# A fused attention and mixing kernel on one core: first loads in two-token runs by halves of the heads, gates eight deep in batch 1, and a new order of instructions

## The chip, the cores and the metric

The kernel runs on one core of one Trainium2 chip. The metric is the device time of one execution in microseconds, with the median of several runs. The profile shows a span that is 1.7 to 1.8 us shorter than this time. All profiles used below are of runs with a granted TensorE clock of 0.995 to 1.0 of full speed.

## The reference, cut to what matters

```python
scores = q @ k.T / sqrt(64) - slope[h] * dist        # 4 batches, 8 heads, 768 tokens, 64 wide
keep = is_global | is_local                          # 8 global tokens, 96 local ones
x = softmax(where(keep, scores, -1e9)) @ v           # heads side by side: (4, 768, 512)
theta = x @ w_theta
u = x + w_tok_r @ (x * cos(theta)) + w_tok_i @ (x * sin(theta))
out = u + relu(u @ w_ch)
```

The kernel works in tiles of 128 tokens. Two tiles make a third of a batch, so there are twelve thirds. Two heads make a pair, and a third has four pairs.

## The kernel before

The program is a table of named operations and a string `ORDER` that lists them in the order in which they are issued; each engine executes its own in that order. The names are short: `t0010` is the transpose of q or k (batch 0, third 0, k = 1, first half), `q000` and `k000` are its evictions from PSUM, `kg` and `kp` write a second copy of k, `sid` is a diagonal, `dtab` a part of the distance table, `etab` a bias table made from it, `bi` the bias matmul of one head, `s` is a pair's scores, `x` the exponential of one head, `v` the product with v, `th` theta, `mx` the token mixing, `ch` the channel mixing. A suffix such as `/ACT` names the engine; `+27` asks for 27 filler matmuls ahead of the operation.

```python
def fill(p_, acc=False):                       # fillers: multiply zeros while TensorE would wait
    for _ in range(plan.pad):
        ...
def load(fn, us, ndesc, spot, depth=0, ...):   # loads with a cast are issued by GpSimd
    ...
    if depth:                                  # the gate: read one element of the load depth back
        add(f"gate{n}", {"POOL": 0.35},
            lambda: nc.gpsimd.tensor_copy(out=scrap, in_=landed[n - depth]()), ...)
    add(f"load{n}", ...)
def first(i, t):                               # q and k of the first third: f32, from SP and ACT
    a = new(st, "e", [T, H, D], FP)
    (nc.sync, nc.scalar)[i].dma_start(out=a,
        in_=(q, k)[i][0, :, t * T:(t + 1) * T, :].rearrange("h p d -> p h d"))
    ...                                        # then a cast to bf16, transposes, evictions
```

Four such first loads bring q and k of 256 tokens: one for each of q, k and tile, all eight heads. A load of one tile has 128 x 8 runs of 64 f32, which is 256 B each.

The softmax here doesn't subtract the row's maximum and nothing guards it: scores larger than these inputs give would overflow.

Of the kernel before, what the change touches and what calls it, by code (L numbers as in the profile page):

```python
# [37 lines left out]
ones6 hw00 hw10 zero rel ones3 tiny hw01 halfpi hw11 warm0 ones5 ones1 ones4 ones2 load1 ones0 ident sid0 far0  # L38
sid2 far1 load2 dtab0 dtab1 dtab2 load3 dtab3 sid4 sid5 etab7 sid1 sid6 sid7 load4 sid3 etab6 bi0000
cast00/DVE bi0001 bi0010 etab3 load5 t0000 cast10/DVE bi0011 q000/DVE etab1 t0010+5 load6 k000/DVE etab2 kg000  # L40
kp000/DVE load7 etab0 cast01/DVE etab5 t0001+27 load8 cast11/DVE etab4 q001/DVE t0011+12 load9 k001/DVE kg001
s000+3 kp001/DVE load10 s001 x0000 x0001 load11 bi0020+3 t0100 x0010 x0011 bi0021 bi0030 load12 q010/DVE t0110
bi0031 s003 k010/DVE load13 s002 x0030 kg010 kp010/DVE x0031 load14 vpa00/DVE x0020 vpb00/DVE x0021 bi0100+6
load15 v003 v000 v001 load16 bi0101 n000 s010 vpa01/DVE load17 bi0110 x0100 bi0111 vpb01/DVE s011 load18 x0101
n003 bi0120 v002 x0110 load19 n001 bi0121 s012 x0111 n002 bi0130 x0120 v010 bi0131 n010 s013 x0121 v011 x0130
v012 n011 t0200 x0131 n012 t0210 q020/ACT bi0200 k020/DVE xt00 bi0201 xc00/ACT bi0210 kp020/DVE bi0211 kg020
v013 vpa02/DVE s020 n013 s021 x0200 vpb02/DVE xt01+6 x0201 bi0220 gate20 x0210 xc01/DVE bi0221+1 load20 v020
x0211 s022 n020 tw00 gate21 x0220 v021 load21 twc00/DVE bi0230 x0221 bi0231 n021 s023 gate22 th000 x0230
load22 x0231 v022 tw10 ts0 gate23 n022 tw11 load23 v023 twc10/DVE th001 n023 gate24 twc11/ACT load24 tw01 xt02
cos000 twc01/DVE gate25 th011 sin000 load25 xc02/DVE cos001 z000 gate26 th010 load26 sin001 th020 z001 cos010  # L50
gate27 load27 sin010 th021 cos011 z010 gate28 t1000 sin011 load28 tw21 cos020 q100/DVE mx000 gate29 sin020
twc21/DVE load29 t1010 cos021 z011 gate30 mx010 sin021 k100/DVE load30 tx1 vpa10/DVE mx001 gate31 kg100 load31
vpb10/DVE z020 mx011 gate32 kp100/DVE load32 z021 tw20 s100 twc20/DVE s101 gate33 mx002 x1000 load33 x1001
x1010 mx012 u00 x1011 gate34 load34 s102 m101 s103 tw30 u01 x1020 gate35 mx020 x1021 m100 load35 x1030 m102
x1031 mx022 gate36 twc30/DVE load36 m103 mx021 gate37 load37 ut00 u02 ut01 uc00/ACT v102 gate38 t1110 uc01/DVE
load38 tw31 k110/DVE ch01 twc31/ACT gate39 kp110/DVE load39 t1100 kg110 o01 v101 v103 q110/DVE gate40 v100
st01 tw41 load40 ch00 n100 twc41/ACT n101 gate41 ut02 load41 tw40 vpa11/DVE uc02/ACT mx030 o00 twc40/ACT
gate42 vpb11/DVE load42 st00 mx032 n102 n103 mx031 gate43 load43 s110 gate44 u03 s111 load44 x1100 t1200 ch02
x1110 gate45 q120/DVE load45 x1101 ut03 x1111 t1210 m110 gate46 uc03/ACT s112 load46 m111 s113 k120/ACT mx040
o02 gate47 x1120 load47 mx041 kp120/DVE st02 x1121 kg120 gate48 x1130 tw51 m112 load48 v110 twc51/ACT tw50  # L60
n110 v111 mx042 gate49 x1131 n111 load49 twc50/ACT vpa12/DVE s120 u04 s121 gate50 x1200 mx050 load50 m113
x1210 vpb12/DVE ut04 x1201 gate51 ch03 uc04/DVE load51 x1211 m120 s122 o03 gate52 s123 x1220 mx051 load52 m121
x1230 st03 v113 x1221 gate53 xt10 n113 load53 x1231 mx052 m122 ts1 gate54 v120 load54 u05 v112 v121 v122 n112
xc10/ACT ut05 gate55 ch04 n120 load55 uc05/DVE th100 vpa20/DVE gate56 m123 load56 ch05 cos100 vpb20/DVE n121
gate57 sin100 v123 load57 xt11 n122 th101 n123 xc11/ACT gate58 load58 o04 xt12 cos101 o05 th110 st04 gate59
sin101 xc12/DVE load59 st05 th111 cos110 z100 gate60 sin110 th121 z101 load60 cos111 z110 th120 sin111 gate61
vpa21/DVE load61 z111 t2100 cos120 t2010 gate62 vpb21/DVE sin120 load62 t2000 q210/DVE cos121 mx110 z120
gate63 sin121 q200/DVE load63 mx111 k200/ACT z121 gate64 t2110 tx2 load64 kg200 mx112 kp200/DVE k210/DVE
gate65 s200 u11 load65 s201 mx100 x2000 kp210/DVE x2001 ut11 kg210 gate66 x2010 mx101 m200 load66 x2011 s202
m201 gate67 s203 t2200 vpa22/DVE load67 x2020 x2021 t2210 vpb22/DVE x2030 q220/DVE v200 gate68 mx102 x2031  # L70
load68 n200 k220/ACT s210 m203 gate69 s211 m202 load69 x2100 mx120 kp220/DVE x2101 u10 gate70 mx122 x2110
load70 m210 x2111 ut10 s212 kg220 gate71 v202 m211 v201 x2120 load71 ch11 n202 x2121 n201 gate72 v203 s213
load72 n203 mx140 x2130 m212 xt20 gate73 x2131 v210 load73 vpa30/DVE s220 n210 v211 x2200 mx121 gate74 n211
x2201 load74 vpb30/DVE s221 m220 s222 gate75 x2210 ch10 load75 u12 x2211 m213 v220 x2220 ut12 mx130 gate76
x2221 m221 load76 s223 n220 v221 gate77 x2230 m222 mx141 load77 x2231 n221 v222 ts2 gate78 v212 m223 mx131
load78 n212 v223 gate79 n222 v213 load79 mx132 n223 n213 gate80 th200 xt22 load80 o11 mx142 vpa31/DVE cos200
gate81 xt21 u13 load81 sin200 ch12 vpb31/DVE u14 gate82 th201 ut13 load82 o12 mx150 o10 cos201 ut14 z200
sin201 mx151 z201 st12 mx152 st11 th221 st10 u15 t3110 ut15 t3010 k310/DVE t3000 k300/DVE t3100 kp310/ACT
th211 q300/DVE q310/ACT kp300/DVE th210 kg300 kg310 vpa32/DVE th220 cos210 vpb32/DVE sin210 t3210 cos211 t3200
z210 ch13 k320/ACT q320/DVE mx200 sin211 kp320/DVE cos220 o13 ch14 sin220 z211 st13 cos221 mx210 z220 sin221  # L80
o14 mx201 tx3 z221 st14 s300 kg320 s301 mx202 x3000 x3010 mx212 x3001 u20 x3011 m300 s302 ut20 s303 m301 ch15
x3020 x3021 x3030 mx211 o15 x3031 s310 m303 st15 s311 u21 x3100 mx220 x3101 m302 ut21 v300 x3110 mx222 m310
x3111 n300 mx221 m311 v301 u22 v303 v302 v310 n302 ch20 ut22 n301 mx230 o20 n303 ch21 st20 n310 xt30 s312 o21
s313 x3120 mx232 x3121 st21 v311 x3130 mx231 n311 x3131 m312 s320 s321 u23 x3200 mx240 x3201 m313 ut23 v312
x3210 ch22 n312 x3211 m320 s322 s323 o22 x3220 mx241 x3230 m321 st22 v313 x3221 mx250 n313 x3231 m322 ts3 v321
xt31 v320 m323 mx252 n320 v322 v323 n321 ch23 n323 th300 n322 o23 xt32 mx242 cos300 sin300 th301 u24 st23 z300
th310 ut24 cos301 sin301 mx251 cos310 z301 th311 sin310 u25 mx300 z310 cos311 ut25 sin311 th320 z311 th321
cos320 sin320 mx301 cos321 z320 ch24 sin321 z321 mx310 o24 mx302 st24 mx312 u30 mx311 ut30 ch25 u31 mx320 ut31
o25 mx322 st25 mx321 ch30 u32 mx330 ut32 o30 mx331 st30 ch31 mx332 o31 mx340 st31 u33 mx341 ut33 mx342 ch32
u34 mx350 ut34 o32 mx352 st32 mx351 ch33 u35 ut35 o33 ch34 uc35/ACT st33 ch35 o34 ch351 o35 st34 o351 st35  # L90
# [5 lines left out]
def kernel(  # L96
# [52 lines left out]
    def act_t(n):  # L149
        return 0.06 + n * 0.00084  # L150
# [11 lines left out]
    DEPTH = 5  # L162
# [58 lines left out]
    def load(fn, us, ndesc, spot, depth=0, reads=(), writes=(), alloc=None):  # L221
        nload[0] += 1
        n = nload[0]
        landed[n] = spot
        after = [f"load{n - 1}"] if n > NFREE else ["hw00"]
        if n == NFREE + 1:
            after = [f"load{i}" for i in range(1, NFREE + 1)]
        if depth:
            add(f"gate{n}", {"POOL": 0.35},
                lambda: nc.gpsimd.tensor_copy(out=scrap, in_=landed[n - depth]()),  # L230
                reads=[("ld", n - depth)], prio=-100 + n - 0.5, after=after)
            after = [f"gate{n}"]
        add(f"load{n}", {"POOL": 0.62 + 0.00028 * ndesc}, fn, reads=reads, writes=list(writes) + [("ld", n)],
            alloc=alloc, prio=-100 + n if n > NFREE else None, lat=(1.05, us + {1: -0.12, 10: 1.1}.get(n, 0.0), 0.65), after=after)
# [39 lines left out]
    def first(i, t):  # L274
# [3 lines left out]
        def fn():  # L278
            a = new(st, "e", [T, H, D], FP)
            (nc.sync, nc.scalar)[i].dma_start(out=a, in_=(q, k)[i][0, :, t * T:(t + 1) * T, :].rearrange("h p d -> p h d"))  # L280

        add(f"hw{i}{t}", {eng: 0.5}, fn, writes=[st], alloc={st: "e"}, prio=-300 + t,
            lat=(0.9, (0.98, 0.7, 1.75, 0.88)[2 * t + i], 1.45), after=["hw00"] if i + t else [])

        def cast():
            if key not in tiles:
                new(key, "qk", [T, 2, 2, DM], BF)
            vector[o.took](out=tiles[key][:, i, t].rearrange("p (h d) -> p h d", d=D), in_=tiles[st])
# [449 lines left out]
```

## Time and profile before

| | before |
|---|---|
| median time | 174.28 us (174.23 to 174.46, 3 runs) |
| profiled span | 172.6 us |
| TensorE busy, with fillers | 162.9 us, 94% |
| VectorE, ScalarE, GpSimd busy | 133.4, 106.0, 85.0 us |
| first exponential starts | 10.39 us |
| last load issued | 100.41 us |

A timeline line has the start, the length of the group, the engine, the line of the kernel, the operation, output and inputs, the count, and in brackets how long the engine stood idle before it and what ended that.

### The profile page before, as it was taken

To read this page: it belongs to the slowest core of one execution; us is meant where nothing else is said; L and a number is where in the kernel's file an instruction comes from. 1 tells how busy PE (TensorE), PEld (TensorE's weight loads), DVE (VectorE), ACT (ScalarE), POOL (GpSimd) and SP (SyncE) were. 2 spreads that over 40 slices of the span, in tenths; PEclk is the share of its full clock that TensorE was granted. 3 is DMA by queue.
4 is the path that set the end of the run, shared out by engine and by line. 5 is a ranking of instruction groups with operands and counts; after the bars stand their busy time and mean duration, and the time that the engine had idled before them with its cause. 6 is when DMAs were issued, how large, how long until landed. Compare 5 with 4: busy or idle time off the path is not lost.

```text
span 172.6 us, 4153 instructions
## 1 busy us (share of the span) xinstructions
PE 162.9 (94%) x1598; PEld 93.2 (54%) x1623; DVE 133.4 (77%) x315; ACT 106.0 (61%) x187; POOL 85.0 (49%) x150
## 2 busy tenths in 40 slices
PE   7998999999997999999999997999999999999991
PEld 2764776555664656565555643654555644444440
DVE  7948886798897698999999994795997975634442
ACT  3954988996445888799877540799518847300010
POOL 8998249779895899898996940000000000000000
PEclk9999999999999999999999999999999999999999
DMA  5999999999999999999999999612335364134334
GB/s 121 188 154 155 188 173 123 143 165 163 157 157 178 184 119 158 113 208 129 132 131 114 165 141 177 219 65 77 105 98 139 104 95 123 48 92 133 93 91 182
DMA packets 96868, 23.73 MB, mean 138 GB/s; under 512 B 91088, under 2 KB 93904, under 8 KB 96848
## 3 DMA queue, kind: packets, MB, share of 16 engines
q0 software_dynamic: 73504, 12.33, 100.7%
q1 hardware_dynamic: 21264, 10.62, 25.1%
q10 hardware_dynamic: 2080, 0.52, 1.7%
q8 instruction: 12, 0.20, 0.5%
q14 instruction: 8, 0.07, 0.1%
HBM read 25.69 MB, written 6.29 MB: 185 GB/s over the span
## 4 chain that ended last, share of the span: by engine, by line
PE 48%; DMA 30%; POOL 6%; DVE 6%; issue 5%; ACT 2%; DVEq 0%; POOLq 0%; SPq 0%; ACTq 0%
PE pb L592 22%; DMA qk<-in_k_dram 10%; PE pb L636 9%; PE pa L549 8%; DMA w_theta_bf<-in_moe_w_theta_dram 5%; DMA qk<-in_q_dram 4%; DMA xT<-x 4%; DMA uT<-u 3%; POOL qk L243 3%; DMA w_ch_bf<-in_moe_w_ch_dram 3%; PE pa L451 3%; PE pa L504 3%; PE pb L371 2%; POOL scrap L230 1%; DVE e L482 1%
## 5 line engine op out<-in xcount | busy, mean ns | idle before, releaser
L592 PE MATMUL pb<-zri,w_tokT 128*128 128x512 bf16 x273 | 67.3, 379 | 1.1 <-issue 0.5
L474 ACT ACTIVATE e<-pa 128x512 bf16<-128x512 f32 (+1 forms) x96 | 46.5, 565 | 20.0 <-PE pa L451 19.4
L592 PEld LDWEIGHTS <-w_tokT 128*128 128x128 bf16 x288 | 26.1, 98 | 28.2
L604 DVE TENSOR_TENSOR u<-x,pb 128x512 bf16<-128x512 bf16 x24 | 16.4, 682 | 11.9 <-PE pb L592 11.7
L636 PE MATMUL pb<-w_ch_bf,uT 128*128 128x512 bf16 (+1 forms) x96 | 24.0, 370 | 0.3
L549 PE MATMUL pa<-w_theta_bf,xT 128*128 128x512 bf16 x93 | 22.5, 379 | 1.3 <-DMA xT<-x 1.1
L482 DVE TENSOR_TENSOR e<-e,etab 128x1024 bf16<-128x1024 bf16 (+1 forms) x36 | 22.4, 639 | 0.4
L257 POOL DMA_DIRECT2D vn<-in_v_dram x24 | 21.8, 910 | 1.4 <-issue 1.4
L558 ACT ACTIVATE cs<-pa,halfpi 128x512 bf16<-128x512 f32 x24 | 16.6, 693 | 9.4 <-PE pa L549 9.2
L243 POOL DMA_DIRECT2D qk<-in_q_dram x22 | 19.6, 891 | 1.9 <-issue 0.9
L570 DVE TENSOR_TENSOR zri<-x,cs 128x1024 bf16<-128x1024 bf16 x24 | 16.2, 685 | 5.0 <-ACT cs L560 4.9
L243 POOL DMA_DIRECT2D qk<-in_k_dram x22 | 19.3, 877 | 0.0
L642 DVE SCALAR_TENSOR_TENSOR o<-pb,u 128x512 f32<-128x512 f32 (+1 forms) x25 | 16.2, 663 | 3.7 <-PE pb L636 3.7
L504 PEld LDWEIGHTS <-e 128*128 128x128 bf16 x352 | 14.5, 98 | 5.2
L517 DVE TENSOR_TENSOR x<-pa,rec 128x256 bf16<-128x256 f32 x36 | 15.3, 425 | 1.2
L620 ACT COPY uT<-pb 128x512 bf16<-128x512 bf16 x4 | 2.4, 594 | 20.9 <-PE pb L616 20.9
L549 PEld LDWEIGHTS <-xT 128*128 128x128 bf16 x96 | 8.9, 98 | 11.5 <-DMA xT<-x 1.6
L371 PE MATMUL pb<-ident,qk 128*128 128x128 bf16 x192 | 14.1, 221 | 1.0 <-DMA qk<-in_k_dram 1.0
L451 PEld LDWEIGHTS <-kk 64*128 64x128 bf16 x352 | 9.9, 94 | 9.3 <-issue 8.0
L451 PE MATMUL pa<-qT,kk 64*128 64x128 bf16 x352 | 14.9, 218 | 0.0
L560 ACT ACTIVATE cs<-pa 128x512 bf16<-128x512 f32 x24 | 14.4, 602 | 0.0
L230 POOL COPY scrap<-qk 1x1 bf16<-1x1 bf16 x33 | 11.3, 343 | 5.1 <-DMA qk<-in_k_dram 2.6
(69 smaller groups left out, 207.2 us busy)
## 6 DMA issues: line engine op xcount, KB each, us to landing
out_dram<-o SPq DMA_DIRECT2D x23, 256.0 KB, 2.3
vn<-in_v_dram POOLq DMA_DIRECT2D x24, 128.0 KB, 5.4
qk<-in_q_dram POOLq DMA_DIRECT2D x22, 128.0 KB, 5.5
qk<-in_k_dram POOLq DMA_DIRECT2D x22, 128.0 KB, 5.3
w_nat<-in_moe_w_tok_r_dram POOLq DMA_DIRECT2D x6, 192.0 KB, 6.0
w_nat<-in_moe_w_tok_i_dram POOLq DMA_DIRECT2D x6, 192.0 KB, 6.5
e<-in_k_dram ACTq DMA_DIRECT2D x2, 256.0 KB, 5.8
e<-in_q_dram SPq DMA_DIRECT2D x2, 256.0 KB, 5.1
```

The lines of the kernel that those rows point to most:

```text
L243: nc.gpsimd.dma_start(out=tiles[key][:, i, t].rearrange("p (h d) -> p h d", d=D), in_=(q, k)[i][b, :, r0:r0 + T, :].rearrange("h p d -> p ...
L257: nc.gpsimd.dma_start(out=v_bufs[i][:, t, :, 0:D], in_=v[b, :, r0:r0 + T, :].rearrange("h p d -> p h d"))
L371: nc.tensor.transpose(p_[:, t - u0, p], tiles[key][:, i, t, p * T:(p + 1) * T], ident)
L451: nc.tensor.matmul(p_[hh][:, s], lhsT=tiles["kk", b, kg][R, kt, p, r, :], rhs=tiles["qT", b, g][R, qt, p, :], start=not biased, stop=not b ...
L474: nc.scalar.activation(tiles[ek][:, hh, 0:n], tiles[pb[hh]][:, 0:n], AF.Exp, scale=scale)
L482: nc.vector.tensor_mul(e_[:, :, 0:n], e_[:, :, 0:n], etab[:, 2 * p:2 * p + 2, s0:s0 + n])
L504: nc.tensor.matmul(o, lhsT=l_, rhs=r_, start=(i == 0), stop=(i == len(mms) - 1))
L549: nc.tensor.matmul(p_, lhsT=tiles["xT", b, g][:, p, t, :], rhs=w_theta_bf[:, p, :], start=(p == 0), stop=(p == NP - 1))
L558: nc.scalar.activation(tiles[ck][:, 0], tiles[ps], AF.Sin, bias=halfpi)
L592: nc.tensor.matmul(p_, lhsT=w_tokT[wi][:, 2 * g + t, tt * T:(tt + 1) * T], rhs=tiles["z", b, g][:, t, wi, :], start=(n == 1 and t == 0 and ...
L604: nc.vector.tensor_add(u.rearrange("n (p c) -> n p c", p=NP), tiles["x", b, tt // 2][:, :, tt % 2, :], tiles[ps].rearrange("n (p c) -> n p ...
L636: nc.tensor.matmul(p_, lhsT=tiles["uT", b, tt][:, p, :], rhs=w_ch_bf[:, p, i * w:(i + 1) * w], start=(p == 0), stop=(p == NP - 1))
```

## The change

Its intent is to shorten the start and to let loads run further ahead. There are four parts. First, each first load takes four heads of all 256 tokens instead of eight heads of 128, and a partition holds two neighbouring tokens, so one run is 512 B. The eviction from PSUM puts the tokens back in order. Second, gates in batch 1 look eight loads back and later gates six, where all looked five back. Third, the diagonals that add the distance bias stay on VectorE, now ahead of the distance table. Fourth, there is a new `ORDER`. Options that are off are cut.

```diff
-    DEPTH = 5
+    DEPTH = 6
+    DEPTH1 = 8
...
-            a = new(st, "e", [T, H, D], FP)
-            ...in_=(q, k)[i][0, :, t * T:(t + 1) * T, :].rearrange("h p d -> p h d"))
+            a = new(st, "e", [T, H // 2, 2 * D], FP)
+            ...in_=(q, k)[i][0, H // 2 * t:H // 2 * (t + 1), 0:2 * T, :].rearrange("h (p j) d -> p h (j d)", j=2))
...
-    batch(1, 0, 0)
-    load_w_tok(2, DEPTH)
+    batch(1, 0, 0, DEPTH1)
+    load_w_tok(2, DEPTH1)
     ... (all loads of batch 1 alike)
+            if halves:
+                vector[o.took](out=d_.rearrange("c t p (n j) -> c t p n j", j=2),
+                               in_=tiles[ps].rearrange("c p j (t n) -> c t p n j", t=2))
...
 ORDER, its start:
-sid2 far1 load2 dtab0 dtab1 dtab2 load3 dtab3 sid4 sid5 etab7 sid1 sid6 sid7 load4 sid3 etab6 bi0000
-cast00/DVE bi0001 bi0010 etab3 load5 t0000 cast10/DVE bi0011 q000/DVE etab1 t0010+5 load6 k000/DVE ...
+sid1 sid0 sid2 load2 sid5 sid6 ident far0 far1 load3 dtab0 dtab1 dtab2 load4 cast00/ACT dtab3 bi0000+1
+cast10/DVE etab5 bi0001 t0000 load5 t0010 q000/ACT bi0010 bi0011 k000/DVE load6 etab7 kg000 cast01/DVE etab4
+load7 kp000/DVE t0001+22 cast11/DVE etab1 s001 q001/DVE t0011 load8 etab0 s000 k001/DVE x0000 ...
```

## The prediction

> **What bounds the kernel now.** I read the page first: busy shares, slices, queues.
>
> ```profile
> PE 162.9 (94%) x1598; PEld 93.2 (54%) x1623; DVE 133.4 (77%) x315; ACT 106.0 (61%) x187; POOL 85.0 (49%) x150
> PE   7998999999997999999999997999999999999991
> DMA  5999999999999999999999999612335364134334
> q0 software_dynamic: 73504, 12.33, 100.7%
> ```
>
> TensorE looks full from end to end, and the DMA engines are full up to slice 25 of 40 (about 108 us) and mostly free after that. The first impression needs a correction: the order of the program holds filler matmuls (a number behind a plus sign), which multiply zeros while TensorE would wait. They count as busy. The groups by shape show them:
>
> ```profile
> L145 PE MATMUL pb<-ident,zero 128*128 128x128 bf16 x50 | 3.5, 219 | 0.0
> L147 PE MATMUL pa<-zero 128*128 128x512 bf16 x6 | 1.8, 378 | 0.5 <-ACT e L474 0.4
> L147 PE MATMUL pa<-zero 128*128 128x384 bf16 x6 | 1.3, 325 | 0.4 <-ACT e L474 0.4
> ```
>
> So I counted useful matmuls, each at the spacing that it has in back-to-back runs of the timeline: 216 ns with 512 columns (8 took 1.90 us, of which the last one's 379 ns is latency), 163 ns with 384, 108 ns with 256 (taken as half of 216), 56 ns for a 128-column transpose (27 fillers in 1.67 us), 34 ns for a score matmul (16 in 0.55 us), 30 ns with 65 columns. 492 x 216 + 8 x 163 + 8 x 108 + 340 x 56 + 352 x 34 + 352 x 30 ns = 150 us. TensorE works from 1.24 to 167.9 us, 166.7 us, so some 16 us of that are warm-up, fillers and waiting. Adding up the same products in stretches of 5 us shows where: by 30 us some 16.8 us of useful work are done, so 13 of the 16 us are lost there. After that the loss grows by about 1.5 us between 55 and 65, by 1 us between 80 and 95 and by 1 us at 105; the remainder is paid back by rounding. **The first 30 us are what can be won**, and the timelines of ScalarE and GpSimd say what limits them:
>
> ```profile
> 4.19 5.12 ACT L682 ACTIVATE etab<-dtab 128x640 bf16<-128x640 bf16 x8 [0.89 <-DVE dtab L207]
> 10.39 1.64 ACT L474 ACTIVATE e<-pa 128x384 bf16<-128x384 f32 x4 [1.07 <-PE pa L451]
> 13.43 1.64 ACT L474 ACTIVATE e<-pa 128x384 bf16<-128x384 f32 x4 [1.40 <-PE pa L451]
> 16.90 4.11 ACT L474 ACTIVATE e<-pa 128x512 bf16<-128x512 f32 x8 [1.83 <-PE pa L451]
> 20.97 1.01 ACT L380 COPY qT<-pb 128x1024 bf16<-128x1024 bf16 x1
> ...
> 18.38 0.53 POOL L269 DMA_DIRECT2D w_nat<-in_moe_w_tok_r_dram  x1 [1.83 <-DMA qk<-in_k_dram]
> 19.30 0.53 POOL L269 DMA_DIRECT2D w_nat<-in_moe_w_tok_i_dram  x1 [0.39 <-DMA qk<-in_q_dram]
> 23.48 0.18 POOL L230 COPY scrap<-w_theta_bf 1x1 bf16<-1x1 bf16 x1 [3.65 <-DMA w_theta_bf<-in_moe_w_theta_dram]
> ```
>
> ScalarE makes all eight bias tables early, then waits three times (4.3 us) for scores. The first score needs all four first loads, which here land between 4.7 and 8.05 us (the issues at line 280 took 4.0 to 6.8 us to land). GpSimd shows a limit that no gate sets: load 18 starts when load 10 has landed and load 19 when load 11 has, so eight loads are outstanding at most. Then comes the first gate, which waits 3.65 us for w_theta, because it asks for the load five before it. Last, the chain that ended last and TensorE's timeline at 55 us:
>
> ```profile
> 49.31 6.74 DMA qk<-in_k_dram
> 99.09 7.33 DMA xT<-x
> ...
> 56.10 0.40 PE L371 MATMUL pb<-ident,qk 128*128 128x128 bf16 x4 [0.97 <-DMA qk<-in_k_dram]
> ```
>
> TensorE waits 0.97 us for the last k load of batch 1, and later for a transposing DMA that shares the queue with the last loads.
>
> **What the Trainium skill says.** "DMA: Bandwidth & Descriptors", Specifications, gives 512 B as the least transfer for line rate; the old first loads move 256 B per head and token, the new ones 512 B. The trace agrees that small packets rule: 91,088 of 96,868 are below 512 B. "Perfetto Trace Analysis", Identifying the Most-Contended Engine, warns that matmul busy time is a poor measure of distance to the roofline; here 94% busy hides 16 us. "VectorE: DVE Perf Modes", Why PSUM operands drop a tier, caps a PSUM source at two elements per cycle, and What auto-detection actually checks asks for step 1 for that; the new evictions of the first third read PSUM with a step of 128 elements, so they should drop to one. In this trace 512 bf16 elements from PSUM at step 1 take 0.42 us, and 512 f32 elements from PSUM (line 642) 0.68 us.
>
> **The change part by part.**
>
> First loads. Four loads of 1,024 packets of 256 B become four of 512 packets of 512 B. In the stationary part of the stream eight loads of 1,024 packets were outstanding and each took about 8.4 us (load 10: issued 9.99, landed 18.38), so one costs the queue 1.05 us, 16.4 ns for each of 64 packets per engine. I take 0.8 us for the new form, an estimate: half the packets, each somewhat longer. Saved: 4 x 0.25 = 1.0 us; the last first load lands at 7.0 instead of 8.05, and everything behind it in the queue about 1.0 us, perhaps up to 2.0 us, sooner.
>
> Halves of the heads. Scores of head pairs 0 and 1 now need only the first q and the first k load, no longer all four. Cost: three evictions on VectorE grow from 0.42 to about 0.66 us (+0.7 us), one moves to ScalarE with one cast (+1.2 us there). The diagonals stay where they were, only earlier than the distance table, so no time comes of them.
>
> New order on ScalarE. Five tables before the first exponential, three between. Walked through with measured durations: table of distances ready on VectorE about 5.2 us, five tables 3.2 us, eviction 0.6 us: first exponential at 9.0 instead of 10.39. Its eight short exponentials (0.41 each) and three tables (0.64) fill the old waits and end near 14.3, where the exponentials of the second third start: 2.6 us before the 16.90 of now. The transposes of the last third need loads 9 to 12, which landed near 20 us and now land near 18 to 19. That caps the gain: **1.2 to 2.8 us, say 2.2, at 30 us**. The fillers say much the same: before 50 x 56 + 6 x 163 + 7 x 216 ns = 5.3 us, after 42 x 56 + 1 x 163 + 5 x 216 ns = 3.6 us, 1.7 us fewer.
>
> Gates eight deep. With eight outstanding allowed anyway, the gates of batch 1 hold nothing back: the 3.65 us behind w_theta go, and the 1.0 us behind w_ch. But the stream is limited by the queue too, so not all of it arrives: by 1.05 us per load and one load per 1.05 us, I put the last k load of batch 1 at 49 to 51 us instead of 56.05. The new order asks for it earlier: the useful work ahead of that transpose is 41.8 us before and 38.7 after. At the speed of the start it would be wanted near 50 us. So this is worth between -1.0 and +1.0 us against the start, +0.3 on average.
>
> The end of the loads (60 to 107 us). Gates of later batches are six deep instead of five, and the stream starts earlier, so the last loads should be out some 3 us sooner and the transposing DMAs near 100 us find a freer queue. Of the 1 us at 105 and the 1 us between 80 and 95 I count 0.5.
>
> Sum: 2.2 + 0.3 + 0.5 = 3.0 us, less 0.1 for small new bubbles. The measured time is 1.7 us longer than the profiled span and I leave that as it is: 174.28 - 2.9 = 171.4 us.
>
> **Rivals.** (1) The load stream binds. The start is capped by loads 9 to 12 at the 1.0 us saved and TensorE then waits at the last k load of batch 1. For it: DMA full to 108 us. Against it: only about 2 us of direct waits on loads now. It would give about 173.2. (2) VectorE binds from 60 to 105 us, where it is busy 43.3 of 45 us; moving a few copies to ScalarE and others back leaves its sum alike. An earlier start then helps only if VectorE's work of the stretch also starts earlier, which it can. Where it does not, some 1.5 us are lost again: 172.8. (3) Deeper gates lengthen each transfer: with eight outstanding a load took 8.4 us, with five 5.4. Stores and transposing DMAs between 85 and 105 us could land later with six outstanding, +0.5 to 1 us: 172.3. (4) All parts add: start 2.8, wait at 55 gone, wait at 105 gone: 169.6.
>
> **Range and chances.** Centre 171.4, with 169.6 from rival 4 and 173.2 from rival 1 as ends. Two per cent is 170.79, so 3.5 us must come; that needs the start near its upper end and one of the later waits gone, about one in three. Slower by 2% would need a new wait of 6 us beside the gain at the start: 0.03.
>
> **What would show it.** First exponential near 9.0 us and the exponentials of the second third near 14.3; waits of ScalarE for scores in the first 20 us below 1.5 us instead of 4.3; first transposes of batch 1 near 32 instead of 34.17; no wait of 3.65 us at a gate; the last k load of batch 1 landing at 49 to 51 us; evictions of the first third at about 0.66 us; the last load issued some 3 us before 100.4. The prediction is wrong if the exponentials start early but TensorE's first work of batch 1 does not, or if a wait of 2 us or more for a load stands near 50 us, or if the gain of the first 30 us is lost between 60 and 107 us.

## The result, and the profile after

The changed kernel took 171.17 us in the median (171.0 to 171.41, 4 runs), the kernel before 174.37 us (174.23 to 177.04, 4 runs) beside it. Ratios here are the mean time of one kernel's fast runs over that of the other's of the same rounds, so not quite the ratio of the medians: 0.982, interval 0.9801 to 0.9839. The run of 177.04 us counts as slow (over 1.5% above the fastest) and is left out of the ratio. The gain is clear of the noise, but by the 2% rule the verdict is "same". The output is correct and the profiled span fell from 172.6 to 169.6 us.

The same rows of the page of the changed kernel:

```profile
PE 162.1 (96%) x1581; PEld 91.9 (54%) x1608; DVE 136.0 (80%) x316; ACT 103.9 (61%) x186; POOL 80.7 (48%) x150
DMA  4999999999999999999999438303363373143334
```

TensorE is as busy as before in a shorter span. The DMA engines are full up to slice 22 (about 93 us) instead of 25. The timeline of ScalarE of the changed kernel, start and length first:

```profile
5.93 0.74 ACT L742 ACTIVATE etab<-dtab 128x640 bf16<-128x640 bf16 x1 [0.77 <-DVE dtab L211]
10.01 0.87 ACT L526 ACTIVATE e<-pa 128x384 bf16<-128x384 f32 x2 [0.36 <-PE pa L499]
14.99 1.08 ACT L526 ACTIVATE e<-pa 128x512 bf16<-128x512 f32 x2
16.34 3.25 ACT L526 ACTIVATE e<-pa 128x512 bf16<-128x512 f32 x6 [0.26 <-PE pa L499]
19.76 1.01 ACT L439 COPY qT<-pb 128x1024 bf16<-128x1024 bf16 x1 [0.17 <-PE pb L425]
```

The first bias table starts at 5.93 us, where it started at 4.19. The first exponential is only 0.38 us sooner, the second third's (14.99 for 16.90) 1.9 us sooner, and the eviction that opens the last third (19.76 for 20.97) 1.2 us sooner. GpSimd of the changed kernel, with its loads and gates:

```profile
17.94 0.53 POOL L273 DMA_DIRECT2D w_nat<-in_moe_w_tok_i_dram  x1 [1.48 <-DMA qk<-in_q_dram]
18.61 0.18 POOL L234 COPY scrap<-qk 1x1 bf16<-1x1 bf16 x1
19.04 0.90 POOL L247 DMA_DIRECT2D qk<-in_q_dram  x1 [0.26 <-issue]
42.41 0.88 POOL L247 DMA_DIRECT2D qk<-in_k_dram  x1
48.42 0.28 POOL L234 COPY scrap<-qk 1x1 bf16<-1x1 bf16 x1
86.22 0.93 POOL L261 DMA_DIRECT2D vn<-in_v_dram  x1
```

The wait of 3.65 us behind w_theta is gone: the first load of batch 1 goes out at 19.04 us, where it went at 24.11. The last k load of batch 1 goes at 42.41 instead of 49.31. The copy at 48.42 is the gate that reads this load, and it did not wait, so the load had landed by then. The last load of all is issued at 86.22 instead of 100.41 us.

Where did the 3.0 us of span come from? Three operations have the same amount of TensorE work ahead of them in both orders, so their times can be compared: the first transpose of batch 1, the last transpose of x in batch 1, and the first theta of batch 3. Their lines from the timeline, before and then after:

```profile
34.17 0.61 PE L371 MATMUL pb<-ident,qk 128*128 128x128 bf16 x8
71.77 0.61 PE L530 MATMUL pb<-ident,x 128*128 128x128 bf16 x8
138.92 1.03 PE L549 MATMUL pa<-w_theta_bf,xT 128*128 128x512 bf16 x4
```

```profile
33.09 0.61 PE L425 MATMUL pb<-ident,qk 128*128 128x128 bf16 x8
70.06 0.61 PE L582 MATMUL pb<-ident,x 128*128 128x128 bf16 x8
135.96 1.03 PE L601 MATMUL pa<-w_theta_bf,xT 128*128 128x512 bf16 x4
```

The gain is 1.1 us at 34 us, 1.7 us at 72 us and 3.0 us at 139 us, and 3.0 at the end. So 1.1 us are of the start, 0.6 us of the stretch with the old wait at 56 us, and 1.3 us came later. In the changed kernel TensorE waits for no DMA for longer than the view of waits lists (0.2 us).

### The profile page after: what moved, and what is told of

Its sections match the earlier page's. It is cut to its first block, busy times and chain, and to the rows that moved or that the text cites. A ratio compares the mean times of both kernels' runs of the same rounds, so it can differ in the third digit from the quotient of the medians.

```text
span 169.6 us, 4122 instructions
## 1 busy us (share of the span) xinstructions
PE 162.1 (96%) x1581; PEld 91.9 (54%) x1608; DVE 136.0 (80%) x316; ACT 103.9 (61%) x186; POOL 80.7 (48%) x150
## 4 chain that ended last, share of the span: by engine, by line
PE 87%; DVE 6%; ACT 2%; issue 2%; DVEq 0%
PE pb L644 37%; PE pa L601 12%; PE pb L688 10%; PE pa L499 7%; PE pb L425 5%; PE pa L556 5%; PE pa L490 3%; PE pb L367 2%; PE pb L582 2%; PE pb L556 2%; ACT e L526 1%; PE pb L668 1%; DVE sid L215 1%; ACT etab L742 1%; DVE kk L384 1%
## 5 line engine op out<-in xcount | busy, mean ns | idle before, releaser
L526 ACT ACTIVATE e<-pa 128x512 bf16<-128x512 f32 (+1 forms) x96 | 47.2, 568 | 25.1 <-PE pa L499 25.0
L610 ACT ACTIVATE cs<-pa,halfpi 128x512 bf16<-128x512 f32 x24 | 16.8, 700 | 7.9 <-PE pa L601 7.8
L261 POOL DMA_DIRECT2D vn<-in_v_dram x24 | 21.2, 892 | 0.6 <-DMA qk<-in_q_dram 0.4
L556 PEld LDWEIGHTS <-e 128*128 128x128 bf16 x352 | 15.0, 98 | 5.8
L499 PE MATMUL pa<-qT,kk 64*128 64x128 bf16 x352 | 15.9, 218 | 0.3 <-DVE qT L436 0.2
L688 PEld LDWEIGHTS <-uT 128*128 128x128 bf16 x100 | 8.9, 98 | 8.8 <-ACT uT L672 0.5
L425 PE MATMUL pb<-ident,qk 128*128 128x128 bf16 x176 | 12.5, 219 | 0.1
```

What stands on the lines that cost most here:

```text
L261: nc.gpsimd.dma_start(out=v_bufs[i][:, t, :, 0:D], in_=v[b, :, r0:r0 + T, :].rearrange("h p d -> p h d"))
L425: nc.tensor.transpose(p_[:, t - u0, p], tiles[key][:, i, t, p * T:(p + 1) * T], ident)
L499: nc.tensor.matmul(p_[hh][:, s], lhsT=tiles["kk", b, kg][R, kt, p, r, :], rhs=tiles["qT", b, g][R, qt, p, :], start=not biased, stop=not b ...
L526: nc.scalar.activation(tiles[ek][:, hh, 0:n], tiles[pb[hh]][:, 0:n], AF.Exp, scale=scale)
L556: nc.tensor.matmul(o, lhsT=l_, rhs=r_, start=(i == 0), stop=(i == len(mms) - 1))
L610: nc.scalar.activation(tiles[ck][:, 0], tiles[ps], AF.Sin, bias=halfpi)
```

## The experiments

The theory after the comparison was: the start gave less than predicted, because VectorE and one needless wait hold it; the gates gave more; and the new order needs the gates. The rivals were that the queue and not the gates limits the loads, that the new loads by themselves are the gain, and that the start has slack later. Between chips the kernel before moved (medians 173.68, 175.46 and 174.79 us).

**Gates back to five.**

```diff
-    DEPTH = 6
-    DEPTH1 = 8
+    DEPTH = 5
+    DEPTH1 = 5
```

> The changed kernel with all gates back at five deep. Theory (the gates are the larger half of the gain): the new order asks for the last k load of batch 1 at 51 us, and with five-deep gates that load lands near 55, so a wait of 2 to 4 us stands there, the last load is issued near 100 us again instead of 86, and the time is 174 to 176 us, no better than the kernel before. Rival (the queue limits the stream, the gates only share it out; the gain is from the start and the order): 171.0 to 172.0 us and no wait above 1 us.

Measured: 173.11 us (172.71 to 173.74), ratio 0.9973 to the kernel before. Its TensorE timeline:

```profile
44.52 0.51 PE L367 MATMUL pb<-ident,w_nat 128*128 128x128 bf16 x6 [0.29 <-DMA w_nat<-in_moe_w_tok_r_dram]
52.49 0.40 PE L425 MATMUL pb<-ident,qk 128*128 128x128 bf16 x4 [0.94 <-DMA qk<-in_k_dram]
```

The waits that the old gates cause are back, at a token weight and at the last k load. They are smaller than expected: 0.9 us and not 2 to 4 (in the later run of this kernel, on another chip, 1.4 us at the token weight and 0.4 us at the k load). The last load goes out at 96.58 us. The time lies between the two forecasts, so the size was missed, though the direction speaks for the gates.

**Gates of batch 1 alone back to five.** Only `DEPTH1 = 5`; later gates stay six deep.

> The changed kernel with five-deep gates for batch 1 alone, six for the later batches as in the changed kernel. If the depth of batch 1 is what counts, the same wait near 51 to 55 us and 173.5 to 175.5 us; if the depth of the later batches is what counts, near 171.5 us.

Measured: 173.12 us (172.39 to 173.34), the same as with all gates at five; a little below the expected range. So with five-deep gates in batch 1, one more load of depth in the later batches shows nothing in the time, although the last load goes out at 93.15 instead of 96.58 us. What the later depth is worth behind eight-deep gates in batch 1 was not run.

**The kernel before with the new depths alone.** The edit is the first and third part of the diff above; loads and order are the old ones.

> The kernel before with the new depths alone (eight for batch 1, six later), old first loads, old order. Theory: the wait of 0.97 us for the last k load at 56 us goes, the load stream ends some 10 us sooner, the wait of 1.1 us for a transposing DMA at 106 us goes too, and the time is 172.0 to 172.8 us. Rival (the old order was fitted to the old arrivals and VectorE binds from 60 to 105 us): 173.5 to 174.3 us.

Measured: 172.51 us (172.07 to 172.72), ratio 0.9931, as the theory said. TensorE no longer waits for the k load at 56 us nor for the transposing DMA of x at 106 us; a wait of 0.6 us for another transposing DMA appears. The last load goes out at 88.50 us.

**The new first loads alone.** The changed kernel with the old order and gates at five.

> The new first loads by halves of the heads, with the old order and the old five-deep gates. Theory: in the old order the first score still comes after all four loads, so only the earlier landing counts: first exponential near 9.9 us instead of 10.39, the wait at 56 us stays, 173.3 to 174.0 us. Rival (the loads by themselves are most of the gain): below 172.5 us.

Measured: 174.59 us (174.21 to 175.46), ratio 1.0071, interval 1.0003 to 1.0139. This is no gain, perhaps a small loss. Both guesses were wrong: the first exponential came later than in the kernel before.

```profile
10.63 1.64 ACT L526 ACTIVATE e<-pa 128x384 bf16<-128x384 f32 x4 [1.32 <-PE pa L499]
```

It starts at 10.63 us and not at 9.9. The groups by shape say why, first of the kernel before, then of the changed one (busy time and mean ns follow the bar):

```profile
L380 DVE COPY kk<-pb 128x512 bf16<-128x512 bf16 x2 | 0.8, 424 | 0.6 <-PE pb L371 0.6
```

```profile
L436 DVE COPY kk<-pb 128x512 bf16<-128x512 bf16 x2 | 1.4, 692 | 0.9 <-PE pb L418 0.5 <-PE pa L499 0.4
```

An eviction that puts tokens back in order takes 692 ns instead of 424. In the old order all four stand ahead of the first exponential, and VectorE's casts do not start sooner, since VectorE is busy with diagonals until 5.2 us. Earlier landing is worth nothing until the order uses it.

**The old order with new loads and gates.** The changed kernel with the old `ORDER` string.

> The changed kernel with the order of the kernel before: new first loads and new gates, old order. Theory: loads and gates together give about 2.5 us and the order another 0.6: 171.4 to 172.4 us. If the order is worth nothing by itself it equals the changed kernel within 0.3 us; if the order is the main thing it is above 173.

Measured: 172.75 us (171.95 to 172.94), ratio 0.9833 to the kernel before on that chip (175.46). It is somewhat above the expected range. The gates alone took 172.51 and 172.66 us, so by these times the new loads add nothing to the gates in the old order, and the rest of the way to 171.2 is the order's, with the halves of the heads on which it relies. But this compares chips: by the ratios to the kernel before (0.9833 here, 0.9931 and 0.9906 for the gates alone) the loads would add over 1 us. The times are the better guide, since two kernels with eight-deep gates repeated within 0.1 us on other chips and the kernel before did not, and the traces agree (see the table of stretches below); a run side by side is missing.

**Runs of 256 B, halves kept.** The loads still bring half of the heads, with one token in a run, and the evictions need no reordering.

```diff
-    a = new(st, "e", [T, H // 2, 2 * D], FP)
-    ...in_=(q, k)[i][0, H // 2 * t:H // 2 * (t + 1), 0:2 * T, :].rearrange("h (p j) d -> p h (j d)", j=2))
+    a = new(st, "e", [T, 2, H // 2, D], FP)
+    for j in range(2):
+        ...out=a[:, j], in_=(q, k)[i][0, H // 2 * t:H // 2 * (t + 1), j * T:(j + 1) * T, :].rearrange("h p d -> p h d"))
```

> The changed kernel, still by halves of the heads and in the same order, but with runs of one token (256 B) instead of two (512 B), as two DMAs for each first load, and evictions of the first third at step 1. Theory (the start hangs on VectorE and ScalarE, not on the landing of the first loads): loads land about 1 us later, evictions fall from 0.69 to about 0.42 us, first exponential between 9.6 and 10.6 us, time 170.9 to 171.7 us. Rival (the earlier landing is what the start gains from): first exponential after 11 us and 172.0 to 172.6 us.

Measured: 171.70 us (171.44 to 172.76). The first exponential is at 10.97 us, 0.96 us later than in the changed kernel and outside what my theory allowed, though the time is at its upper end. Three lines of its timeline:

```profile
4.94 1.28 ACT L294 ACT_TABLE_LOAD   x1 [4.94 <-DMA e<-in_q_dram]
6.91 0.62 PE L419 MATMUL pb<-ident,qk 128*128 128x128 bf16 x8 [0.98 <-ACT qk L294]
8.72 0.88 DVE L294 CAST qk<-e 128x512 bf16<-128x512 f32 x1 [0.24 <-DMA e<-in_q_dram]
```

Evictions did fall to 424 ns, but two things come later. ScalarE's table load of 1.28 us, which the changed kernel does at 1.88 us while the loads are under way, stands here behind the wait for a load, so its cast starts at 6.23 instead of 4.54 us, the transposes at 6.91 wait for it, and ScalarE has its five tables at 10.47 instead of 9.66 us. And VectorE's cast of the second half of q waits for its load until 8.72 us; the eviction behind it, for which pair 0 waits, ends at 10.51 instead of 9.65 us. Only the second is the landing of a load. So the landing takes part at the start, against my theory, but how much of the 0.96 us it makes by itself is not shown: by these times the table load alone would cost 0.8 us, and a load in two DMAs also costs a second issue of about 0.5 us on SP and ACT. About half of the 0.96 us reaches the end (171.70 us here, 171.2 for the changed kernel on other chips).

**The scores of pair 0 earlier.** In the changed kernel, `s000` stands behind `q001`. Its TensorE and VectorE timelines:

```profile
8.33 0.59 PE L499 MATMUL pa<-qT,kk 64*128 64x128 bf16 x6
8.96 0.69 DVE L436 COPY qT<-pb 128x512 bf16<-128x512 bf16 x1
9.29 0.23 PE L499 MATMUL pa<-qT,kk 64*128 64x128 bf16 x2
9.71 0.29 PE L499 MATMUL pa<-qT,kk 64*128 64x128 bf16 x4 [0.18 <-DVE qT L436]
```

The first two matmuls of pair 0 run at 9.29 us and the other four wait until the eviction at 8.96 has ended. By the code they do not read what it writes: it writes pairs 2 and 3 of both tiles, they read pair 0 of the second tile, which lies between those columns in the buffer. That the dependence is taken from the range of addresses is my reading; what the next run shows is that it can be avoided.

```diff
-... t0001+22 cast11/DVE etab1 s001 q001/DVE t0011 load8 etab0 s000 k001/DVE x0000 ...
+... t0001+22 cast11/DVE etab1 s001 s000 q001/DVE t0011 load8 etab0 k001/DVE x0000 ...
```

> The changed kernel with the scores of head pair 0 issued directly after those of pair 1, ahead of the eviction of the second half of q. In the changed kernel four of its matmuls waited for that eviction, which writes other columns of the same buffer. Theory: they start near 8.9 instead of 9.71 us, the first exponential moves from 10.01 to about 9.7, and 0.2 to 0.4 us come off the time: 170.8 to 171.1. Rival (the start has slack further on): 171.2 within 0.1.

Measured: 170.52 us (170.51 to 170.54), ratio 0.9715 on that chip. In its timelines the twelve score matmuls run together and the first exponential starts at 9.56 us:

```profile
8.33 0.76 PE L446 MATMUL pa<-qT,kk 64*128 64x128 bf16 x12
9.56 0.86 ACT L473 ACTIVATE e<-pa 128x384 bf16<-128x384 f32 x2
```

It is faster than expected.

**Diagonals later as well.** As the run before, and six of the eight diagonals moved behind the first casts, `kp000` ahead of `cast01`.

```diff
-... load1 tiny sid4 sid3 sid7 sid1 sid0 sid2 load2 sid5 sid6 ident far0 far1 ...
+... load1 tiny sid1 sid0 load2 ident far0 far1 ... (sid2 and 3 behind cast10, 4 and 5 behind k001, 6 and 7 behind kp001)
```

> As the run before, and six of the eight diagonals moved from ahead of the distance table to gaps of VectorE behind the first casts, and the first twin copy ahead of the third cast. Theory (VectorE's work ahead of the distance table holds up the start): tables start at 5.2 instead of 5.93 us, first exponential near 9.0, and most of this 1 us comes through: 170.1 to 170.7 us. Rival (the second and last third are held by the loads or by TensorE and ScalarE together): first exponential near 9.0 but 170.9 to 171.3 us.

Measured: 170.53 us (170.47 to 170.79). The first exponential is at 8.86 us, 0.7 us sooner than in the run before, and no time came off against that run: the rival's case. The time lies in the range given for the theory only because the run before was faster than expected. Its timelines of ScalarE and TensorE show where it went:

```profile
8.86 0.86 ACT L473 ACTIVATE e<-pa 128x384 bf16<-128x384 f32 x2
14.42 0.19 PE L503 MATMUL pb<-vp,e 128*128 128x65 bf16 x1 [0.26 <-DVE vp L407]
15.86 3.25 ACT L473 ACTIVATE e<-pa 128x512 bf16<-128x512 f32 x6 [0.68 <-PE pa L446]
```

At 14.42 us TensorE waits for VectorE's second copy of v, and the six exponentials that follow start at 15.86 us, where the run before has them at 15.87. So the diagonals ahead of the table do hold up the first exponential, but VectorE's copies hold the next stage at the same place.

**The four main kernels on one chip.** To put sizes beside one another, the changed kernel and three of the above ran again, five rounds each.

> The changed kernel itself once more, so that it stands on the same chip as the three others; the kernel before moved by 2 us between chips. Both theories: 171.0 to 171.6 us, with the kernel before 2 to 4 us above it.

> The changed kernel with five-deep gates, again, now beside the changed kernel. Theory (gates carry about half of the gain, because with the old ones the last k load of batch 1 comes too late for the new order): 1.3 to 2.3 us above the changed kernel of this call. Rival (the difference of the first run was the chip's): within 0.5 us of it.

> The kernel before with the new depths alone, again, beside the changed kernel. Theory: about half of the way, 1.0 to 1.8 us above the changed kernel and 1.2 to 2.2 below the kernel before. Rival (the new depths alone bring nearly all): within 0.5 us of the changed kernel.

> The scores of head pair 0 ahead of the eviction of the second half of q, again, beside the changed kernel. Theory (a wait that the buffer's layout makes and no data needs, 0.4 us, is on the path to the end): 0.4 to 0.8 us below the changed kernel of this call, outside its spread. Rival (the difference was the chip's): within 0.2 us.

| kernel | median, all runs | mean of fast runs | ratio to before, 95% interval |
|---|---|---|---|
| before | 174.79 (173.46 to 178.06) | 174.42 | |
| before with new depths | 172.66 (172.38 to 172.95) | 172.64 | 0.9906 (0.9863 to 0.9948) |
| changed, gates at five | 173.90 (171.90 to 174.72) | 173.32 | 0.9942 (0.9879 to 1.0005) |
| changed | 171.20 (170.98 to 171.61) | 171.21 | 0.9821 (0.9782 to 0.9859) |
| changed, `s000` early | 170.55 (170.52 to 170.72) | 170.59 | 0.9785 (0.9747 to 0.9822) |

The means are of the runs marked fast (nine of eleven of the kernel before, four of six of the changed one with gates at five, all of the others). The new depths alone bring 174.42 - 172.64 = 1.8 us. The loads and the order without them bring 174.42 - 173.32 = 1.1 us. Both bring 3.2 us, so the parts about add up, though the interval of the second reaches 1. Putting the old gates into the changed kernel costs 173.32 - 171.21 = 2.1 us, within what the theory asked for (2.7 us by the medians of all runs). The reordered version is 0.6 us below the changed kernel, and the two sets of runs do not overlap. With the later diagonals (170.53 us on another chip) it is the fastest of all that ran.

The traces split these sums by stretch. The three operations compared above cut the time of TensorE into three; each row is one fast execution, in us:

| kernel | to the first transpose of batch 1 | on to the last of x in batch 1 | on to the first theta of batch 3 |
|---|---|---|---|
| before | 34.17 | 37.60 | 67.15 |
| before with new depths, two chips | 34.11, 34.24 | 36.45, 36.45 | 66.46, 66.22 |
| new loads, old order and gates | 34.28 | 37.86 | 66.60 |
| new loads and gates, old order | 34.27 | 36.45 | 66.65 |
| changed, gates at five, two chips | 32.98, 32.97 | 38.43, 39.39 | 65.90, 65.94 |
| changed, two chips | 33.09, 32.97 | 36.97, 36.72 | 65.90, 66.17 |

The start gains 1.1 us with the new order, whatever the gates, and nothing in the old order with new loads or gates. In the middle the new depths gain 1.15 us in the old order, and taking them from the changed kernel costs 1.5 to 2.7 us. In the last stretch the new order has its whole gain of 1.2 us with the old gates too, so with this order the depths add nothing there. In the old order the depths show 0.7 to 0.9 us, but the new loads alone already show 0.55, so differences of half a microsecond between single executions are not to be read.

The spread may be a result too. The fast runs of the two kernels with five-deep gates lie 2.0 us (before) and 2.1 us apart, those of the three with eight-deep gates 0.2 to 0.6 us. This is a tendency and not a rule: the fast runs lie 0.95 to 2.4 us apart with five-deep gates in batch 1, but 0.23 us in the three of the kernel before in the first comparison; with eight-deep gates 0.03 to 0.99 us, but 1.32 us for the runs of 256 B. That the gates cause it is not shown.

## Why the prediction was right or wrong, point by point

The predicted time was 171.4 us and 171.17 came, but three of its four terms were off and they made up for each other: 2.2, 0.3 and 0.5 us were forecast, and 1.1, 0.6 and 1.3 us came. That the sum was right is luck.

- **The start** was to give 2.2 us, at the least 1.2. It gave 1.1 us at the first transpose of batch 1. Three steps failed. "No time comes of them" was wrong for the diagonals: all eight stand on VectorE ahead of the distance table, where two did before, and the first bias table came at 5.93 us and not at 5.2 (to which the walk had moved it from 4.19 without saying for what). So ScalarE had its five tables at 9.66 and not at 9.0 us. The run with later diagonals confirms this link (8.86 us). The walk also missed the wait of pair 0, with which the first exponential came at 10.01 us; it is worth 0.45 us there and 0.6 us in the end. Last, the gain of 1.9 us at the second third shrank to 1.2 us by the last third; the waits of 0.26 and 0.17 us on the way are in the timeline, and in the run with later diagonals VectorE's copies hold this stage.
- **What caps the start** was named wrongly. Loads 9 to 12 were to hold it. Load 11 had landed when GpSimd went on at 17.94 us and load 12 when its gate at 18.61 did not wait, and the transposes that need them were not on TensorE before 19.1.
- **First loads.** The estimate of 0.8 us for a load and 1.0 us saved held: the last of the four took 5.7 us from issue to landing, where it took 6.8. The eviction at about 0.66 us was 0.69. By itself this brought nothing in the old order with the old gates (174.59 us, 173.68 for the kernel before).
- **Fillers.** Their count fell by the 1.7 us computed, but as a hint at the gain of the start (1.1 us) it was too high by half. A slip in the count of lost time: 16.8 us of useful work by 30 us leave 12 us lost since 1.24 us, not 13, which counts from zero.
- **Gates in batch 1** were to give 0.3 us net and gave about 0.6 by the landmarks; in the old order they gave 1.15 us in that stretch. The term that was mis-sized is the landing of the last k load: 49 to 51 us forecast, by 48.42 measured. I had let the queue take back part of the head start of the loads. It took nothing back: the first load of batch 1 went out 5.1 us sooner and the last k load 6.9 us sooner. One part did not come: GpSimd still waits for w_ch at a gate, 1.11 us.
- **The end of the loads** was to give 0.5 us with the last load 3 us sooner. It was 14.2 us sooner, and the gain after 72 us was 1.3 us. The wait of 1.1 us for the transposing DMA, which shared the queue with the last loads, is gone. It also went in the old order when only the gates changed, but likewise in the new order with the old gates (last load at 96.58 us), where the stretch after 72 us is as short as in the changed kernel. So the freer queue, from which the prediction took this gain, is not what gave it, as far as these single executions show: the new order is.
- **Rivals.** A load stream that binds was real, but for the old gates only: with them the new order waits again. VectorE as the bound from 60 to 105 us is not shown: it is busy 41.2 of these 45 us now, where it was 43.3. Longer transfers from deeper gates did not hurt; a load of q took 5.7 us to land in the median, for 5.5 before (but 7.9 us for `w_tok_r`, for 6.0).

What stays open: how the new order avoids the wait for the transposing DMA, whether the new order would gain at the start without the halves of the heads (no such run was made), and what the length of the runs is worth by itself, since the 256 B runs also moved a table load and added an issue.

## What to carry to other kernels

A gate that throttles loads is to be checked against the slowest thing it waits for: here one look at a large weight load, five loads back, stopped all loads behind it for 3.65 us, and with gates that look further back the time fell by 1.2 and 1.8 us. A load that landed earlier was worth something here only where the order of instructions asked for it earlier and the engine that receives it was free. Busy fillers and waits between two halves of one buffer hide in a busy share of 94%, so count useful work and look at what ended each small wait.

## What the Trainium skill lacked or had wrong

- "DMA: Bandwidth & Descriptors" gives 512 B as the least transfer for line rate. It has no measured time for the same load with runs of 256 B and of 512 B on this chip. Here halving the packets of the four first loads brought the last landing from 6.8 to 5.7 us after issue.
- The same page gives no number of loads that a program like this one has outstanding at most. Here load 18 waited for load 10 and load 19 for load 11, eight in both kernels and ahead of any gate; the trace does not tell why.
- No page that I read treats the scatter of runs of one kernel. In the last call the fast runs span 173.46 to 175.45 us for the kernel before and 170.98 to 171.61 us for the changed kernel on the same chip; the cause is not shown.
